# One more attention block turned by the DMA: block (0, 3), with another order of the first chunk and two copies on ScalarE

## The chip, the cores and the metric

The kernel runs on one core of a Trainium2 chip. The metric is the device time of one execution in microseconds (us). The kernel before has a median of 2323.25 us over three runs (2319.2 to 2325.48). Engines are named as in the profile: PE is TensorE (PEld its weight loads), DVE is VectorE, ACT is ScalarE, POOL is GpSimd, SP is SyncE, which issues most DMAs.

## The reference

Eight batches of 2496 tokens go through an attention without softmax; its output, 19968 rows of 256, goes through a mixture of eight experts with one expert for each row.

```python
scores = (1.0 / S) * np.matmul(z, z.transpose(0, 2, 1))   # z: 8 x 2496 x 64
attn = np.maximum(scores, 0.0) ** 2
x = u * np.matmul(attn, v)                                # u, v: 8 x 2496 x 256
logits = x @ w_gate                                       # 8 experts
...
h = np.maximum(xe @ w1[e], 0.0)                           # 256 -> 1024
ye = h @ w2[e]                                            # 1024 -> 256
out[mask] = gate_w[mask, None] * ye
```

Queries and keys are the same tensor z, so `attn` is symmetric: the part of keys a against queries b is the transpose of the part of keys b against queries a. All is float32 in and out.

## The kernel before, in words

The kernel has two parts, attention and then the experts. Only the attention is touched.

**Tiling.** A batch b (0 to 7) has five chunks c of 512 queries (the last has 448), and its keys are taken in ten pairs kp of 256 keys (two tiles of 128), so that key chunk cc = kp // 2. One step is (b, c, kp): `scores` makes the weights of 256 keys against the chunk's queries, and `weighted` multiplies them into the two PSUM accumulators of the chunk (`acc`, L343 to L346), with 12 products of 512 columns. Each float32 operand is split into a high part and a remainder (`hi`, `lo`; tiles `thi`, `tlo`), which is why a step needs three products for each pair of tiles.

**Where weights come from.** On and above the diagonal (cc >= c) four products of z make them (L306, L307, tile `ps_s`), ACT does Relu (L315) and Square (L316), and DVE makes `hi` (L317) and `lo` (L319). Below the diagonal (cc < c) nothing is computed again: the block stored by the earlier chunk is transposed. That is done in one of two ways, chosen by `by_dma`:

- By PE: the block is kept as float32 in a slot (tile `s`), eight transposes of 128x128 with the identity (L278) put it into PSUM, ACT makes `hi` (L279), DVE `lo` (L280).
- By the DMA: when the block is made, its 16-bit high halves are copied by ACT (L330) and its low halves by DVE (L331) into a ring of three tiles `th`, and SP issues a DMA_TRANSPOSE into the slot (L332). When it is used, ACT puts the high halves together (L263), DVE the low ones (L264), ACT makes `hi` (L265) and DVE `lo` (L266). No PE work is in it.

Before the change blocks (0, 1), (0, 2), (1, 2), (1, 3), (2, 3) and (3, 4) go by the DMA; (0, 3), (0, 4), (1, 4) and (2, 4) by PE. On the diagonal a chunk's second pair takes half of its weights from four PE transposes of the first (L312).

**Order.** `order_of` gives the order of the key pairs in a chunk. In the first chunk of batches 1 to 7 it is 0, 2, 6, 3, 7, 4, 8, 5, 9, 1: pairs that go by the DMA (2 to 5) take turns with the others, and the second diagonal pair (1) is last. Scores run three steps ahead of `weighted` (two in batch 0, whose first chunk has the order 0 to 9 and also splits z and v). The framework's scheduler then sets the order of each engine's instructions; engines keep it, so an instruction that waits holds up all behind it on its engine or queue. Other work goes in between: after a chunk `gate_x` makes x (L366, L376, L377), its halves are copied (L385, L386) and turned by four small DMA transposes on SP (L390), then the row goes to memory (L471). The last chunk of a batch also loads v of the next one (SP, L134) and splits it (ACT L139, DVE L140). Rings bound how far things run ahead: `ps_s` has two buffers, `tf` (the weights before their split) three, `thi` and `tlo` four each, slots six.

Of the kernel before, what the change touches and what calls it, by code (L numbers as in the profile page):

```python
# [47 lines left out]
def fused_kernel(ctx: ExitStack, tc: tile.TileContext, zt, ut, v, wg, wcat, out):  # L48
    nc = tc.nc
# [6 lines left out]
    NC_ = len(chunks)  # L56
# [38 lines left out]
    def ring_halves():  # L95
        return sb.tile([P, 4, QC], U16, name="th", tag="th", bufs=3)
# [128 lines left out]
    def order_of(b, c):  # L225

        kps = list(range(NKP))
        if b and c in (0, NC_ - 1):
            kps.append(kps.pop(1))
        elif 0 < c < NC_ - 1:  # L230
            kps.append(kps.pop(2 * c + 1))
        if b or c:

            ways = [[kp for kp in kps if kp // 2 > c and by_dma(c, kp // 2) == w] for w in (True, False)]
            at = [i for i, kp in enumerate(kps) if kp // 2 > c]
            mixed = []
            while any(ways):
                for w in ways:
                    if w:
                        mixed.append(w.pop(0))  # L240
            for i, kp in zip(at, mixed):
                kps[i] = kp
        return kps
# [3 lines left out]

    def by_dma(c, cc):

        return c < cc < NC_ - 1 and (c, cc) != (0, 3) or (c, cc) == (NC_ - 2, NC_ - 1)  # L250

    def scores(b, c, kp):
        q0, n = chunks[c]
        cc = kp // 2
        hi, lo = ring_hi(), ring_lo()
        if by_dma(min(c, cc), max(c, cc)) and cc < c:

            i, st = stored[b, cc, c]
            a = ring_f()
            st = st.rearrange("p k (i h j) q -> p h j (k i) q", i=2, h=2)  # L260
            dst = a.bitcast(U16).rearrange("p j (r q h) -> p h j r q", q=P, h=2)
            js = slice(kp % 2 * 2, kp % 2 * 2 + 2)
            nc.scalar.copy(dst[:, 1], st[:, 0, js])  # L263
            (nc.scalar.copy if c == NC_ - 1 else nc.vector.tensor_copy)(dst[:, 0], st[:, 1, js])  # L264
            nc.scalar.copy(hi[:, :, :n], a[:, :, :n])  # L265
            nc.vector.tensor_tensor(lo[:, :, :n], a[:, :, :n], hi[:, :, :n].bitcast(F32), op=ALU.subtract)  # L266
            if kp % 2:
                del stored[b, cc, c]
                free.insert(len(free) - len(weights), i)
            return hi, lo  # L270
# [15 lines left out]
        if cc > c:  # L286
            if kp % 2 == 0:
                i = free.pop(0)
                if by_dma(c, cc):
                    st = slot(i).bitcast(U16).rearrange("p (k r q) -> p k r q", k=2, q=P)  # L290
                else:
                    st = slot(i).rearrange("p (k i q) -> p k i q", k=2, i=2)
                stored[b, c, cc] = i, st
            a = ring_f() if by_dma(c, cc) else stored[b, c, cc][1][:, kp % 2]
        elif late and kp % 2 == 0:
            sd = ring_sd().bitcast(F32).rearrange("p s r -> p (s r)")[:, 0:2 * QC]
            a = stored[b, c, c] = sd.rearrange("p (i n) -> p i n", i=2)
        else:
            a = ring_f()
# [26 lines left out]
        if by_dma(c, cc):  # L326

            th = ring_halves().rearrange("p (i h) n -> p i h n", h=2)
            src = a.bitcast(U16).rearrange("p i (n h) -> p i n h", h=2)
            nc.scalar.copy(th[:, :, 0, :], src[:, :, :, 1])  # L330
            nc.vector.tensor_copy(th[:, :, 1, :], src[:, :, :, 0])  # L331
            nc.sync.dma_start_transpose(out=stored[b, c, cc][1][:, kp % 2], in_=th.rearrange("p i h n -> p (i h n)"))  # L332
        return hi, lo

# [486 lines left out]


    steps = [(b, c, kp) for b in range(B) for c in range(NC_) for kp in order_of(b, c)]
    LAST = len(steps) - 1
    LA = 3
    ZF, ZS = (0, 2), (1, 4)
    LP = 2
    ready, accs = {}, {}
    ready[0] = scores(*steps[0])
    split_v(0, 0)  # L830
    split_z(0, 1)
    pinned(lambda: warm_up(4))
    ready[1] = scores(*steps[1])
    pinned(lambda: warm_up(8))
    bg.extend([constants] + [nothing] * 6 + [gate_parts])
# [13 lines left out]
    for s, (b, c, kp) in enumerate(steps):  # L849
# [16 lines left out]
        def score():  # L866
            ready[ahead] = scores(*steps[ahead])
# [7 lines left out]
        if c == NC_ - 1 and b + 1 < B:  # L875

            for i in ((0, 1) if j == 0 else (j + 1,) if j < NKP - 1 else ()):
                fetch_v(b + 1, order_of(b + 1, 0)[i])
            if j:
                pinned(lambda: split_v(b + 1, order_of(b + 1, 0)[j - 1]))  # L880
# [122 lines left out]
```

## Time and profile before

| | |
|---|---|
| median of three runs | 2323.25 us |
| the profiled execution | 2324.7 us, span 2322.9 us |
| attention, up to about 1381 us | PE busy 1373.67, DVE 1078.71, ACT 982.21 us |
| experts, the 942 us after it | PE busy 905.19, DVE 553.28, ACT 483.08 us |
| DMA engines, mean share | 0.61 in the attention, 0.54 in the experts |
| PE transposes L278 | x512, 104.7 to 1368.8 us |
| DMA transposes into slots, L332 | x96 |

A batch takes about 170 us (batch 3 runs from about 522 to 692 us), its chunks 30 to 37 us each. The time of a matmul in a row of the profile (about 390 ns for 512 columns) is its latency; matmuls are started every 0.23 us and overlap. So the cost of a PE instruction is read from one start to the next. On ACT and DVE rows without idle time overlap as well, by about 0.1 us.

### The profile page before, as it was taken

The page shows a single profiled execution, that of the slowest core. Times are in us where ns is not written, and L with a number is a line of the kernel's source. Part 1 is how long each engine was busy: PE and PEld are TensorE (multiplying, and loading weights), DVE is VectorE, ACT ScalarE, POOL GpSimd, SP SyncE. Part 2 cuts the span into 40 slices and gives each one's busy share as a digit, 9 for nine tenths or more (in the row PEclk, how much of TensorE's full clock was granted, in tenths as well). Part 3 has the DMA queues.
Part 4 walks back from the last instruction along what each step waited for, and adds up shares of the span by engine and source line. Part 5 has one row for each costly group of instructions (what it writes and reads, how often), then busy time and mean ns, then how long its engine had stood idle before and what let it go on. Part 6 is the DMA issues. An engine that isn't in the chain of part 4 may idle for free.

```text
span 2322.9 us, 33688 instructions
## 1 busy us (share of the span) xinstructions
PE 2278.9 (98%) x12320; PEld 1925.6 (83%) x12320; DVE 1632.0 (70%) x2909; ACT 1465.3 (63%) x1985; POOL 625.7 (27%) x626
## 2 busy tenths in 40 slices
PE   9999999999999999999999989899999999999998
PEld 7888888888888888888888877688888888888887
DVE  8868868878778778877878766455566656657554
ACT  8768668677677777767776654355465555546454
POOL 1011111112102102102111244543445435345322
PEclk9999999999999999999999999899999999999999
DMA  6556656657567367467375484654566646457620
GB/s 163 104 92 135 97 86 135 93 95 134 85 105 132 80 116 121 79 118 125 79 114 95 121 176 89 189 123 131 154 152 173 176 128 207 134 146 194 151 89 29
DMA packets 454366, 287.31 MB, mean 124 GB/s; under 512 B 389100, under 2 KB 411130, under 8 KB 444976
## 3 DMA queue, kind: packets, MB, share of 16 engines
q1 hardware_dynamic: 422800, 165.98, 40.0%
q0 software_dynamic: 31392, 119.10, 17.6%
q8 instruction: 98, 1.61, 0.4%
q14 instruction: 76, 0.62, 0.1%
HBM read 149.79 MB, written 43.43 MB: 83 GB/s over the span
## 4 chain that ended last, share of the span: by engine, by line
PE 85%; issue 4%; DMA 3%; ACT 3%; DVE 2%; POOL 1%; another core or an unknown queue 1%; SPq 0%; POOLq 0%; ACTq 0%
PE ph L776 16%; PE acc L343 13%; PE acc L346 13%; PE acc L345 13%; PE y L799 11%; PE y L802 6%; PE ps_s L306 4%; PE ps_s L307 4%; DMA vr<-in_v_dram 2%; PE ps_s L278 2%; PE pt L398 1%; POOL out_dram L815 1%; PE ps_s L312 1%; DMA rows<-xrows,laidx 1%
## 5 line engine op out<-in xcount | busy, mean ns | idle before, releaser
L346 PE MATMUL acc<-thi,t 128*128 128x512 f32 (+1 forms) x1600 | 614.3, 386 | 0.0
L343 PE MATMUL acc<-thi,t 128*128 128x512 f32 (+1 forms) x1600 | 608.0, 392 | 1.1 <-issue 0.7
L345 PE MATMUL acc<-tlo,t 128*128 128x512 f32 (+1 forms) x1520 | 586.0, 386 | 0.1
L781 DVE SCALAR_TENSOR_TENSOR t<-ph,t 128x512 fp32r<-128x512 f32 (+1 forms) x328 | 220.3, 675 | 238.1 <-ACT t L780 192.5
L776 PE MATMUL ph<-thi,t 128*128 128x512 f32 (+2 forms) x1248 | 379.3, 361 | 3.8 <-issue 2.1
L780 ACT ACTIVATE t<-ph 128x512 fp32r<-128x512 f32 (+1 forms) x328 | 191.9, 591 | 289.1 <-PE ph L776 210.4
L346 PEld LDWEIGHTS acc<-thi,t 128*128 128x128 f32 x1600 | 300.2, 188 | 55.3 <-DVE t L140 0.6
L343 PEld LDWEIGHTS acc<-thi,t 128*128 128x128 f32 x1600 | 299.5, 188 | 54.4 <-DVE x L366 1.2
L345 PEld LDWEIGHTS acc<-tlo,t 128*128 128x128 f32 x1520 | 285.6, 188 | 50.8 <-DVE tlo L319 0.7
L476 POOL DMA_INDIRECT lst<-toks,posi x160 | 197.0, 1231 | 468.2 <-DVE posi L468 425.8
L799 PE MATMUL y<-t,t 128*128 128x512 f32 x1062 | 306.3, 397 | 13.5 <-DVE t L734 6.4
L776 PEld LDWEIGHTS ph<-thi,t 128*128 128x128 f32 x1248 | 226.1, 189 | 32.9 <-issue 2.9
L799 PEld LDWEIGHTS y<-t,t 128*128 128x128 f32 x1062 | 191.5, 191 | 48.7 <-ACT t L780 7.8
L776 PE MATMUL ph<-tlo,t 128*128 128x512 f32 (+2 forms) x624 | 225.6, 362 | 0.7 <-issue 0.7
L815 POOL DMA_INDIRECT out_dram<-tf,lfidx x136 | 143.7, 1057 | 273.4 <-DVE tf L813 245.5
L802 PEld LDWEIGHTS y<-t,t 128*128 128x128 f32 x1062 | 175.8, 190 | 35.2 <-DVE t L781 5.7
L802 PE MATMUL y<-t,t 128*128 128x256 f32 x1062 | 185.0, 283 | 3.6 <-DVE t L781 3.6
L315 ACT ACTIVATE tf<-ps_s 128x1024 f32<-128x1024 f32 (+1 forms) x145 | 133.8, 923 | 85.3 <-PE ps_s L307 43.3
L307 PE MATMUL ps_s<-t,t 128*128 128x512 f32 (+1 forms) x480 | 178.9, 376 | 0.0
L380 POOL MEMSET rows<- 128x64 int32 x40 | 6.8, 172 | 581.7 <-DMA xrows<-rows 359.6
L317 DVE CAST thi<-tf 128x1024 fp32r<-128x1024 f32 (+1 forms) x145 | 90.9, 627 | 102.3 <-ACT tf L316 94.5
L711 POOL DMA_INDIRECT rows<-xrows,lfidx x136 | 138.9, 1021 | 50.2 <-issue 38.3
(252 smaller groups left out, 4050.2 us busy)
## 6 DMA issues: line engine op xcount, KB each, us to landing
vr<-in_v_dram SPq DMA_DIRECT2D x80, 256.0 KB
xrows<-rows SPq DMA_DIRECT2D x32, 544.0 KB
u<-in_ut_dram SPq DMA_DIRECT2D x32, 512.0 KB
zr<-in_zt_dram SPq DMA_DIRECT2D x38, 256.0 KB
u<-in_ut_dram SPq DMA_DIRECT2D x8, 448.0 KB
xrows<-rows SPq DMA_DIRECT2D x8, 408.0 KB
rows<-th SPq DMA_TRANSPOSE x160
lst<-toks,posi POOLq DMA_INDIRECT x160
```

The costliest lines, as they stand in the source:

```text
L307: nc.tensor.matmul(ps[:, i, m:n], lhsT=hl_k, rhs=lh_q[:, m:n], start=False, stop=True)
L343: nc.tensor.matmul(acc[d][:, :n], lhsT=vh, rhs=hi[:, i, :n], start=first and i == 0, stop=False)
L345: nc.tensor.matmul(acc[d][:, :n], lhsT=vh, rhs=lo[:, i, :n], start=False, stop=False)
L346: nc.tensor.matmul(acc[d][:, :n], lhsT=vl, rhs=hi[:, i, :n], start=False, stop=last and i == 1)
L476: i = nc.gpsimd.indirect_dma_start(out=lst1, out_offset=bass.IndirectOffsetOnAxis(ap=posi[:m, j:j + 1], axis=0), in_=toks[:m, col + j:col ...
L711: nc.gpsimd.indirect_dma_start(out=xg[:, s, :], out_offset=None, in_=src, in_offset=bass.IndirectOffsetOnAxis(ap=lists[which]["idx"][:, s, ...
L776: nc.tensor.matmul(o, lhsT=w1[:, part, dd, fs], rhs=xx[:, dd, :n], start=p == 0, stop=p == 5)
L780: nc.scalar.activation(hh[:, :m], ph[:, :m], AF.Relu)
L781: nc.vector.scalar_tensor_tensor(hl[:, :m], ph[:, :m], 0.0, hh[:, :m].bitcast(F32), op0=ALU.max, op1=ALU.subtract)
L799: nc.tensor.matmul(y, lhsT=h[:, cs], rhs=w2[:, f % 2].rearrange("p i d -> p (i d)"), start=f == 0, stop=False)
L802: nc.tensor.matmul(y[:, 0:D], lhsT=h[:, cs], rhs=w2[:, f % 2, 0, :], start=False, stop=f == NF - 1)
L815: d = nc.gpsimd.indirect_dma_start(out=out, out_offset=bass.IndirectOffsetOnAxis(ap=lists[which]["idx"][:, s, t:t + 1], axis=0), in_=yo[:, ...
```

## The change

Three lines. Block (0, 3), made in the first chunk (pairs 6 and 7) and used in the fourth (pairs 0 and 1), goes by the DMA in all eight batches. The order of the first chunk in batches 1 to 7 becomes 0, 2, 3, 1, 4, 5, 8, 6, 9, 7: the second diagonal pair is fourth. And in those first chunks the low halves of pairs 2 and 3 (block (0, 1)) are copied by ACT and no longer by DVE.

```diff
     def order_of(b, c):
         kps = list(range(NKP))
-        if b and c in (0, NC_ - 1):
+        if b and c == 0:
+            return [0, 2, 3, 1, 4, 5, 8, 6, 9, 7]
+        if b and c == NC_ - 1:
             kps.append(kps.pop(1))
         elif 0 < c < NC_ - 1:
             kps.append(kps.pop(2 * c + 1))
...
     def by_dma(c, cc):
-        return c < cc < NC_ - 1 and (c, cc) != (0, 3) or (c, cc) == (NC_ - 2, NC_ - 1)
+        return c < cc < NC_ - 1 or (c, cc) == (NC_ - 2, NC_ - 1)
...
             nc.scalar.copy(th[:, :, 0, :], src[:, :, :, 1])
-            nc.vector.tensor_copy(th[:, :, 1, :], src[:, :, :, 0])
+            (nc.scalar.copy if b and c == 0 and kp < 4 else nc.vector.tensor_copy)(th[:, :, 1, :], src[:, :, :, 0])
```

Lines after the edit stand two further down: L278 is L280 in the changed kernel, L315 is L317, L330 is L332, L343 is L345. In its instruction lists, L333 is the copy of low halves on either engine.

Three places show how the instructions stand. First PE in batch 3, near the end of the third chunk, where the scores of the fourth chunk's first pair are due. Before:

```order
L345 MATMUL acc1_6029<-tlo_6134,t4_5252 128x512
L346 MATMUL acc1_6029<-thi_6133,t4_5252 128x512
L278 MATMUL ps_s_6263<-ident_97,s2_5314 128x128 x8
L343 MATMUL acc0_6028<-thi_6164,t4_5184 128x512
L345 MATMUL acc0_6028<-tlo_6165,t4_5184 128x512
```

In the change, at the end of the same chunk (no L278 stands between its products any more):

```order
L345 MATMUL acc1_6033<-thi_6202,t4_5333 128x512
L348 MATMUL acc1_6033<-thi_6202,t4_5333 128x512
L308 MATMUL ps_s_6447<-t2_5145 128x512
L309 MATMUL ps_s_6447<-t2_5146,t2_5145 128x512
L308 MATMUL ps_s_6447<-t2_5145 128x512
```

The eight transposes of block (0, 3) are gone; the next scores that PE makes are those of the fourth chunk's diagonal pair 6, which now stand before the third chunk's last products.

Second, ACT in the last part of the first chunk of batch 3, from the Relu of pair 8 on. Before (`s1_5475` holds pairs 8 and 9, `tf_5506` pair 5, `ps_s_5557` the diagonal pair 1, `sd_5659` the next chunk's diagonal, `s0_5259` block (0, 1)):

```order
L315 ACTIVATE s1_5475<-ps_s_5474 128x1024
L315 ACTIVATE tf_5506<-ps_s_5505 128x1024
L316 ACTIVATE s1_5475<-s1_5475 128x1024
L385 COPY th_5496<-x_5338 128x1024
L316 ACTIVATE tf_5506<-tf_5506 128x1024
L315 ACTIVATE s1_5475<-ps_s_5533 128x1024
L330 COPY th_5515<-tf_5506 128x2x512
L316 ACTIVATE s1_5475<-s1_5475 128x1024
L313 CAST thi_5555<-ps_s_5557 128x2x256
L315 ACTIVATE sd_5659<-ps_s_5658 128x1024
```

In the change (`s3_5480` holds pairs 8 and 9, `tf_5512` pair 6, `tf_5564` pair 7, `s0_5253` block (0, 1)):

```order
L317 ACTIVATE s3_5480<-ps_s_5479 128x1024
L317 ACTIVATE tf_5512<-ps_s_5510 128x1024
L318 ACTIVATE s3_5480<-s3_5480 128x1024
L387 COPY th_5501<-x_5336 128x1024
L318 ACTIVATE tf_5512<-tf_5512 128x1024
L317 ACTIVATE s3_5480<-ps_s_5539 128x1024
L332 COPY th_5521<-tf_5512 128x2x512
L317 ACTIVATE tf_5564<-ps_s_5563 128x1024
L265 COPY tf_5601<-s0_5253 128x1024
L318 ACTIVATE s3_5480<-s3_5480 128x1024
L318 ACTIVATE tf_5564<-tf_5564 128x1024
```

The half pair 1 has left this stretch and the whole pair 7 has come in, and a copy for the next chunk (L265) stands ahead of the Squares of pairs 9 and 7.

Third, ACT where the fourth chunk's last score (its second diagonal pair) is followed by the last chunk's first. Before (`ps_s_6589` is the first score of the last chunk, `s2_6487` block (3, 4)):

```order
L316 ACTIVATE tf_6551<-tf_6551 128x2x256
L279 CAST thi_6587<-ps_s_6589 128x2x448
L263 COPY tf_6760<-s2_6487 128x1024
L264 COPY tf_6760<-s2_6487 128x1024
L263 COPY tf_6813<-s2_6487 128x1024
L264 COPY tf_6813<-s2_6487 128x1024
L428 ACTIVATE ex_6361<-dl_6580 128x32
```

In the change (`ps_s_6581` is the first score of the last chunk, `s5_6479` block (3, 4)):

```order
L318 ACTIVATE tf_6543<-tf_6543 128x2x256
L265 COPY tf_6752<-s5_6479 128x1024
L266 COPY tf_6752<-s5_6479 128x1024
L265 COPY tf_6805<-s5_6479 128x1024
L266 COPY tf_6805<-s5_6479 128x1024
L281 CAST thi_6579<-ps_s_6581 128x2x448
L430 ACTIVATE ex_6353<-dl_6572 128x32
```

The four copies of block (3, 4), which wait for its DMA, now stand ahead of the cast that the last chunk's first products need.

## The prediction, made before the changed kernel ran

> **What bounds the kernel now.** I read the page's busy shares first, then busy time by stage, then the groups by line, then the order of time at the places that the edit touches.
>
> ```profile
> PE 2278.9 (98%) x12320; PEld 1925.6 (83%) x12320; DVE 1632.0 (70%) x2909; ACT 1465.3 (63%) x1985; POOL 625.7 (27%) x626
> PEclk9999999999999999999999999899999999999999
> 0.00:1381.00 1381.00, 1373.67 (x7477) 1148.62 (x7477) 1078.71 (x1867) 982.21 (x1128) 225.93 (x240) 1.00 0.61 111
> ```
>
> The third row is a window (columns: length, then busy time of PE, PEld, DVE, ACT, POOL, granted clock, DMA share, GB/s). In the attention PE idles 7.3 us of 1381 at full clock. Time falls here if PE work falls, provided the work put elsewhere hides behind PE. Batch 3 by chunks:
>
> ```profile
> 522.60:559.30 36.70, 36.70 (x188) 30.37 (x188) 28.44 (x48) 28.79 (x34) 7.27 (x5) 1.00 0.66 130
> 559.30:592.10 32.80, 32.80 (x175) 27.05 (x174) 28.95 (x51) 24.67 (x29) 4.40 (x5) 1.00 0.88 120
> 592.10:624.60 32.50, 32.50 (x182) 26.93 (x181) 27.04 (x49) 23.21 (x28) 5.04 (x5) 1.00 0.57 90
> 624.60:660.70 36.10, 36.10 (x206) 30.01 (x205) 23.71 (x40) 24.69 (x27) 4.16 (x5) 1.00 0.36 82
> ```
>
> PE is without a gap in all four; DVE and ACT have 4 to 12 us to spare in each.
>
> **What PE loses.** Block (0, 3) is two groups of eight transposes in each batch, 16 groups in all. One group in order of time, and ahead of it a step's 12 products:
>
> ```profile
> 643.93 0.39 PE L343 MATMUL acc<-thi,t 128*128 128x512 f32 x1
> ...
> 646.65 0.28 PE L306 MATMUL ps_s<-t 128*128 128x256 f32 x1
> ...
> 650.09 0.39 PE L346 MATMUL acc<-thi,t 128*128 128x512 f32 x1
> 650.32 1.03 PE L278 MATMUL ps_s<-ident,s 128*128 128x128 f32 x8
> 651.11 0.48 PE L343 MATMUL acc<-thi,t 128*128 128x512 f32 x1
> 651.42 0.40 PE L345 MATMUL acc<-tlo,t 128*128 128x512 f32 x1
> ```
>
> From start to start, 12 products take 2.72 us, one 0.227. From the group's start to the start of the second product after it are 1.10 us; less that product's 0.23 the group costs 0.87 us. 16 x 0.87 = 13.9 us less on PE. Nothing is added there.
>
> [...]
>
> **What ACT and DVE gain.** Durations of one, by shape:
>
> ```profile
> L263 ACT COPY tf<-s 128x1024 uint16<-128x1024 uint16 x96 | 126.7, 1359 | 31.7 <-DMA s<-th 17.9 <-DVE tlo L266 11.0 <-ACT thi L279 2.5
> L330 ACT COPY th<-tf 128x1024 uint16<-128x1024 uint16 x96 | 100.5, 1047 | 1.6 <-DMA s<-th 0.2
> L265 ACT CAST thi<-tf 128x1024 fp32r<-128x1024 f32 x80 | 83.0, 1056 | 56.6 <-PE acc L346 43.5 <-DVE tlo L266 5.0 <-DVE tf L264 4.3
> L279 ACT CAST thi<-ps_s 128x1024 fp32r<-128x1024 f32 x16 | 16.2, 1015 | 0.0
> L331 DVE COPY th<-tf 128x1024 uint16<-128x1024 uint16 x96 | 66.1, 689 | 0.6
> L264 DVE COPY tf<-s 128x1024 uint16<-128x1024 uint16 x80 | 57.9, 754 | 0.0
> ```
>
> *First chunk, batches 1 to 7.* ACT: high halves of pairs 6 and 7 (2 x 1.05), and low halves of pairs 2 and 3 (not seen on ACT; the nearest row is L330, the same shape and stride, 1.05 each): 4.2 us more. DVE: two low halves more, two fewer: 0. Is there room? ACT in batch 3, the stretch with its idle time and the one after it:
>
> ```profile
> 533.45 1.05 ACT L330 COPY th<-tf 128x1024 uint16<-128x1024 uint16 x1
> 540.85 1.03 ACT L315 ACTIVATE s<-ps_s 128x1024 f32<-128x1024 f32 x1 [6.35 <-PE ps_s L307]
> 542.68 1.06 ACT L316 ACTIVATE s<-s 128x1024 f32<-128x1024 f32 x1
> 548.32 0.58 ACT L313 CAST thi<-ps_s 128x512 fp32r<-128x512 f32 x1
> 551.98 0.58 ACT L315 ACTIVATE tf<-ps_s 128x512 f32<-128x512 f32 x1
> 554.87 0.63 ACT L316 ACTIVATE tf<-tf 128x512 f32<-128x512 f32 x1
> 540.80:560.00 19.20, 19.20 (x91) 16.01 (x90) 13.28 (x20) 18.07 (x20) 0.00 (x0) 1.00 0.38 75
> ```
>
> ACT idles 6.35 us because the scores of pair 8 come late in PE's order, then works 18.07 of 19.20 us. In the change's order the low halves of pairs 2 and 3 and the half pair 1 fall ahead of that hole, which covers them. In the tight stretch the half pair 1 goes (0.58 + 0.58 + 0.63 = 1.8), and pair 7 comes in whole (Relu 1.03, Square 1.06, high half 1.05: 3.1), pair 6 in the place of pair 5: 1.3 more, against 1.1 of idle time. What is pushed out at the end is work for the next chunk, which has 8 us to spare (second row by chunks, 32.80 - 24.67). Pair 9 is the tightest. From the start of pair 8's scores, PE's order is: scores of 8 and 6 (8 x 0.227 = 1.8), products of pair 5 (2.7), scores of 9 and 7 (1.8), products of 8 (2.7), a score (0.9), products of 6 (2.7), a score (0.9), then those of 9, at 13.6. ACT starts at 0.9 and has, in the order shown with the change, four times 1.0 to 1.1 up to the Square of 6 (6.1 with the row copy), Relu 9, high half 6, Relu 7 (9.2), L263's kind 1.36, Square 9: 11.7; DVE needs 3 x 0.69 more: 13.7. That is level with PE, and pair 7, in the same way, is 0.5 us ahead; ACT's rows overlap by about 0.1 us when none waits, which gives back near 1. I take 0. Ends: 0 (PE has no gap there to lose) and all 4.2 us uncovered, 7 x 4.2 = 29.4.
>
> *Fourth chunk, all batches.* Per pair ACT has L263 and L265 for L279 (1.36 + 1.06 - 1.02 = 1.4), DVE L264 more (0.75; the subtraction costs the same from either memory). 2.8 and 1.5 us per batch, beside 5.5 to 12.4 us of spare time on either engine in the third and fourth rows by chunks (the fourth chunk's first scores run in the third's stretch). PE, which runs ahead there, needs none of it sooner. 0; ends 0 and 8 x 2.8 = 22.4.
>
> *Batch 0, first chunk.* Here the low halves stay on DVE, and nothing moves away:
>
> ```profile
> 19.60:39.60 20.00, 20.00 (x88) 15.94 (x87) 19.28 (x27) 17.84 (x22) 0.00 (x0) 1.00 0.95 197
> ```
>
> DVE is busy 19.28 of 20.00 us. Two low halves are 2 x 0.69 = 1.4 us on the path; ACT's 2.1 just fit its 2.2 us of idle time. +1.4; ends 0 and 1.4 + 2.1 = 3.5.
>
> **What the DMA gains.** 16 transposes. The rows of SP's issue and of the waits on them:
>
> ```profile
> L332 SPq DMA_TRANSPOSE s<-th x96: 1317/2074/5038, 16.8 to 1333.8; - x96
> ACT tf L263 <- DMA s<-th: 17.9, 8, 4.3
> ACT t L139 <- DMA vr<-in_v_dram: 28.7, 12, 5.6
> ```
>
> SP issues one in 2.07 us: 4.1 us per batch of 170. Behind the two on SP's queue stand u, z and the next chunk's transposes, for which later chunks wait; in batch 0 also the last v. The first chunk's end and the second's start have a free DMA (0.38 in the 540.80 row). The result is read two chunks later. 0; the existing waits bound it: 28.7 us if v came late as often again.
>
> **The fourth chunk's end.** The cast and the subtraction of a first score of the last chunk:
>
> ```profile
> L279 ACT CAST thi<-ps_s 128x896 fp32r<-128x896 f32 x48 | 42.6, 902 | 48.9 <-PE acc L346 44.7 <-PE ps_s L278 4.2
> L280 DVE TENSOR_TENSOR tlo<-ps_s,thi 128x896 fp32r<-128x896 f32 x48 | 52.1, 1087 | 55.1 <-ACT thi L279 46.0 <-issue 9.1
> ```
>
> There ACT's order puts four copies of block (3, 4) ahead of the cast that the last chunk waits for. Each batch waits once for that block's DMA (17.9 us over 8, longest 4.3). The block is made earlier than before (its scores start in the third chunk now), so the wait should shrink. Once PE ends the fourth chunk's last diagonal transposes, it has 2.72 us of products and 0.87 of the last chunk's first transposes; ACT has 0.58 + 0.58 + 0.63 before it reaches the copies, 1.8 us ahead of the transposes' end. 8.6 us of PE work (2.72 + 2.27 + 0.87 + 2.72) follow. Copies (4 x 1.36), cast (0.90) and subtraction (1.09) take 7.4 us and end 1.8 + 8.6 - 7.4 = 3.0 us ahead. 0; ends: all of PE's idle time in the attention gone, -7.3, or +1.3 per batch (below).
>
> **Sum.** -13.9 + 1.4 = -12.5 on the profiled 2324.7 gives 2312.2. That execution lies 1.45 over the median, so 2311 for the median of 2323.25.
>
> **Rivals.**
> - *ACT becomes the bound of the first chunk* (slower). For it: 18.07 of 19.20 us, and weights that come level with PE; whatever ACT is late there, PE is late. Against it: the hole of 6.35 us. Price: 29.4 uncovered, 2323.25 - 12.5 + 29.4 = 2340; it cancels the gain from 12.5 / 7 = 1.8 us per batch, and decides for slower from 2.8.
> - *The copies at the fourth chunk's end hand it back* (no change). With a wait of 4.3 us in every batch the first weights come 4.3 - 3.0 = 1.3 us late, 10 in all: 2321. Against it: the mean wait was 2.2 us, and the block is earlier.
> - *The DMA is late instead* (no change): 0.88 of the DMA is used in the second chunk, 0.95 in batch 0. If a sixth more transposes bring a sixth more of both waits (46.6 / 6 = 7.8): 2319. [...]
> - *Waits go too* (faster than forecast): the earlier block (3, 4) frees ACT, and with it v's queue; PE's idle 7.3 us goes: 2304.
>
> **How the numbers follow.** A run of this kernel spreads by 0.3% (7 us), about what can be told from no change. Forecast 0.56, waits go too 0.10, copies 0.13, DMA 0.09, ACT 0.12. Faster by over 0.3% (under 2316.3): 0.56 + 0.10 = 0.66. Within: 0.13 + 0.09 = 0.22. Slower: 0.12. The range leaves out the slower case and the ends of the others: 2302 (13.9 + 7.3 below the median) to 2322 (just past the copies). The forecast's own is 2305 to 2316.
>
> **What would show it.** L280 with 384 instructions for L278's 512, L334 with 112 for 96; PE still without gaps in the attention, which ends some 12 us earlier, with batches 1 to 7 near 168.3 us (1.74 less) and batch 0 hardly shorter. Wrong, if ACT's rows end the idle time of L343 or L345 at the end of first chunks, if the cast L281 does at the start of last ones, or if the waits on `th` or v grow by more than 8 us.

## The result, and the profile after

The change made the kernel slower: 2335.98 us (median of 14 runs, 2326.24 to 2343.96) against 2323.64 us for the kernel before on the same chip, a ratio of 1.0051, 95% interval 1.0036 to 1.0067. Forecast were 2311 us, with a range of 2302 to 2322. The profiled execution of the changed kernel took 2336.84 us with a span of 2335.1.

First the page's busy times, and then the attention as one window, of after and of before (columns: length, then PE, PEld, DVE, ACT, POOL, granted clock, DMA share, GB/s):

```profile
PE 2276.6 (97%) x12192; PEld 1916.9 (82%) x12192; DVE 1643.8 (70%) x2927; ACT 1510.3 (65%) x2031; POOL 623.6 (27%) x626
0.00:1393.70 1393.70, 1370.98 (x7338) 1138.59 (x7339) 1087.23 (x1876) 1025.72 (x1170) 225.34 (x240) 0.99 0.68 115
```

```profile
0.00:1378.10 1378.10, 1371.36 (x7465) 1147.28 (x7466) 1075.81 (x1858) 980.30 (x1125) 225.93 (x240) 1.00 0.61 111
```

The 128 transposes are gone (12320 to 12192), and yet the attention ends 15.6 us later, at 1393.7. The experts take 941.4 us after it (944.8 before), so between these two executions the whole loss lies in the attention. PE's idle time there rose from 6.7 to 22.7 us, and its busy time fell by only 0.4 us: rows that start late one by one, or at a lower clock, count as busy (in the 3.40 us from 382.5 on, at a granted clock of 0.50, nine rows make PE busy for all of it). Lost time is therefore better read from one start to the next. I added up by how much each interval between two starts exceeds that of an undisturbed neighbour (0.227 us for 512 columns, 0.203 for 448, 0.119 for 256, 0.109 for a transpose), where it is over 0.06 us:

| us lost by PE | before | after |
|---|---|---|
| first chunks, batch 0 / batches 1 to 7 | 3.1 / 1.3 | 4.4 / 10.6 |
| second and third chunks, batches 1 to 7 | 5.2 | 5.6 |
| fourth chunks, batches 1 to 6 / batch 7 | 4.7 / 2.6 | 15.7 / 10.2 |
| last chunks, batches 1 to 7 | 8.3 | 5.9 |
| whole attention | 26.8 | 54.2 |

(Batch 0's other chunks, 1.5 and 1.8 us, are in the last row alone. A stall at the end of a fourth chunk reaches into the last one, so these two rows are best read together: 15.6 us before, 31.8 after.) So 27.4 us of new lost time stand against 13.9 us of saved work: +13.5 of the 15.6 us. Not all of it is waiting. In the change's attention the granted clock of PE is 0.50 in four stretches, 20.5 us in all (rows in the last section), and there is no such stretch in the attention of the trace of before; the slower starts in them, waits aside, make some 7 of the 54.2 us. Who waits is in the table of waits of the changed kernel (us in all, times, longest):

```profile
ACT tf L265 <- DMA s<-th: 36.1, 8, 12.3
ACT t L139 <- DMA vr<-in_v_dram: 18.8, 12, 4.1
ACT th L332 <- DMA s<-th: 17.2, 7, 3.9
DVE th L333 <- DMA s<-th: 13.5, 6, 3.5
PE ps_s L308 <- ACT tf L317: 5.7, 5, 2.2
PE acc L345 <- ACT thi L281: 4.6, 3, 2.7
```

The first row was 17.9 us with a longest of 4.3, the third 0.2, the fourth not there. The wait for v fell from 28.7 to 18.8. In the groups by line, the cast and the subtraction of the last chunk's first scores show the same:

```profile
L282 DVE TENSOR_TENSOR tlo<-ps_s,thi 128x896 fp32r<-128x896 f32 x48 | 51.5, 1086 | 80.3 <-ACT thi L281 80.3
L281 ACT CAST thi<-ps_s 128x896 fp32r<-128x896 f32 x48 | 43.4, 903 | 55.2 <-PE ps_s L280 31.8 <-PE acc L348 22.7 <-issue 0.7
```

DVE waits 80.3 us for the cast L281, where it was 46.0.

**End of a fourth chunk.** Batch 2 in order of time, ACT and then PE (start, length, in brackets the idle time before and what ended it):

```profile
482.19 0.63 ACT L318 ACTIVATE tf<-tf 128x512 f32<-128x512 f32 x1
488.94 1.35 ACT L265 COPY tf<-s 128x1024 uint16<-128x1024 uint16 x1 [6.12 <-DMA s<-th]
492.55 1.32 ACT L266 COPY tf<-s 128x1024 uint16<-128x1024 uint16 x1
493.74 0.89 ACT L281 CAST thi<-ps_s 128x896 fp32r<-128x896 f32 x1
```

```profile
482.12 1.03 PE L280 MATMUL ps_s<-ident,s 128*128 128x128 f32 x8
491.64 0.39 PE L348 MATMUL acc<-thi,t 128*128 128x512 f32 x1
494.68 0.47 PE L345 MATMUL acc<-thi,t 128*128 128x448 f32 x1 [2.65 <-ACT thi L281]
495.81 1.97 PE L280 MATMUL ps_s<-ident,s 128*128 128x128 f32 x8 [0.66 <-DVE tlo L282]
```

The first transposes of the last chunk are in PSUM at 483.2 us. ACT could cast them at once, but block (3, 4)'s four copies stand ahead of the cast in its list, and they wait 6.12 us for the block's DMA. PE has finished the fourth chunk at 491.9 and then waits. Before, one cast stood ahead of the copies:

```profile
481.60 0.89 ACT L279 CAST thi<-ps_s 128x896 fp32r<-128x896 f32 x1
483.49 1.35 ACT L263 COPY tf<-s 128x1024 uint16<-128x1024 uint16 x1 [1.00 <-DMA s<-th]
```

Count both from the chunk's first product (456.4 us before, 460.2 after). ACT came to the copies after 26.1 us and found the block there after 27.1; in the change it comes after 22.6 and finds it after 28.7. In all of batches 0 to 6 ACT came after 25.9 to 26.1 us, and comes after 22.6 to 23.9, one cast sooner and in a chunk that takes 31.7 us for 34.3 where PE does not wait. The first copy starts after 27.9 us before and 26.5 in the change (means). So the block is not later there, and the wait still grows from 1.9 to 3.4 us in the mean. Only in batch 7 does the block itself come late, after 34.7 us for 29.0 (there the copies stood ahead of both casts before, too). SP in batch 2, after and then before:

```profile
464.27 12.52 SPq L392 DMA_TRANSPOSE rows<-th  x4
476.90 8.57 SPq L334 DMA_TRANSPOSE s<-th  x2
```

```profile
470.68 5.23 SPq L390 DMA_TRANSPOSE rows<-th  x4
476.08 1.79 SPq L332 DMA_TRANSPOSE s<-th  x1
479.16 2.91 SPq L332 DMA_TRANSPOSE s<-th  x1
```

SP takes 12.52 us over four small transposes that took 5.23, and then 8.57 over the two of the block that took 4.7. All the same it is done with them 25.3 us after the chunk's first product, for 25.6 before, because it comes to them earlier. Over all, the median issue of one into a slot rose from 2.07 to 2.98 us.

**First chunks.** Batch 2 again, ACT and the PE row that waits for it:

```profile
379.25 1.04 ACT L332 COPY th<-tf 128x1024 uint16<-128x1024 uint16 x1 [3.95 <-DMA s<-th]
380.21 1.02 ACT L317 ACTIVATE tf<-ps_s 128x1024 f32<-128x1024 f32 x1
```

```profile
381.28 0.50 PE L308 MATMUL ps_s<-t,t 128*128 128x512 f32 x1 [2.18 <-ACT tf L317]
```

A copy into the ring of three `th` waits until an earlier DMA transpose has read its buffer. The Relu behind it is late, the PSUM buffer of the score comes free late, and PE waits 2.18 us.

**The end of batch 7.** There PE stops, with nothing in the trace that it waits for:

```profile
1350.90 0.39 PE L347 MATMUL acc<-tlo,t 128*128 128x512 f32 x1 [1.04 <-issue]
1353.96 0.58 PE L348 MATMUL acc<-thi,t 128*128 128x512 f32 x1 [2.67 <-issue]
1356.05 0.58 PE L345 MATMUL acc<-thi,t 128*128 128x512 f32 x1 [1.50 <-issue]
```

```profile
1344.00:1350.00 6.00, 5.75 (x33) 4.74 (x32) 1.98 (x7) 0.74 (x2) 3.85 (x5) 1.00 1.65 74
1350.00:1356.00 6.00, 0.97 (x2) 0.57 (x2) 0.00 (x0) 0.00 (x0) 0.00 (x0) 0.65 1.11 237
1356.00:1362.00 6.00, 5.82 (x18) 3.86 (x18) 0.00 (x0) 4.89 (x5) 0.00 (x0) 0.50 0.09 19
1362.00:1368.00 6.00, 5.80 (x35) 5.01 (x34) 5.09 (x13) 2.64 (x5) 2.52 (x3) 0.99 0.65 217
```

In 6 us PE starts two products; then it runs at a granted clock of 0.50 (18 of its rows in 6 us, 33 in the window two before). It happens beside eight gathers of token rows for the experts that POOL issues from 1337.9 to 1349.7 (L713) and the transposes of block (3, 4).

### The profile page after: what moved, and what is told of

It reads as the page before. It is cut to its first block, busy times and chain, and to the rows that moved or that the text cites. A ratio compares the mean times of both kernels' runs of the same rounds, so it can differ in the third digit from the quotient of the medians.

```text
span 2335.1 us, 33566 instructions
## 1 busy us (share of the span) xinstructions
PE 2276.6 (97%) x12192; PEld 1916.9 (82%) x12192; DVE 1643.8 (70%) x2927; ACT 1510.3 (65%) x2031; POOL 623.6 (27%) x626
## 3 DMA queue, kind: packets, MB, share of 16 engines
q8 instruction: 97, 1.59, 0.3%
## 4 chain that ended last, share of the span: by engine, by line
PE 78%; DMA 7%; issue 5%; DVE 4%; ACT 3%; POOL 1%; another core or an unknown queue 1%; SPq 0%; POOLq 0%; DVEq 0%; ACTq 0%
PE ph L778 16%; PE acc L345 12%; PE acc L348 12%; PE acc L347 11%; PE y L801 11%; PE y L804 6%; DMA s<-th 5%; PE ps_s L308 4%; PE ps_s L309 4%; PE ps_s L280 1%; PE pt L400 1%; DVE tlo L321 1%; DMA rows<-xrows,laidx 1%; ACT tf L265 1%; ACT tf L266 1%
## 5 line engine op out<-in xcount | busy, mean ns | idle before, releaser
L345 PE MATMUL acc<-thi,t 128*128 128x512 f32 (+1 forms) x1600 | 604.8, 392 | 6.5 <-ACT thi L281 4.6
L345 PEld LDWEIGHTS acc<-thi,t 128*128 128x128 f32 x1600 | 301.3, 189 | 62.3 <-ACT thi L281 6.5
L317 ACT ACTIVATE tf<-ps_s 128x1024 f32<-128x1024 f32 (+2 forms) x161 | 149.3, 932 | 72.0 <-DVE tlo L316 42.1
L265 ACT COPY tf<-s 128x1024 uint16<-128x1024 uint16 x112 | 147.7, 1363 | 36.1 <-DMA s<-th 36.1
L319 DVE CAST thi<-tf 128x1024 fp32r<-128x1024 f32 (+2 forms) x161 | 103.0, 640 | 91.4 <-ACT tf L318 87.8
```

The source lines that it names most:

```text
L317: nc.scalar.activation(a[:, :, m:n], ps[:, :, m:n], AF.Relu)
L345: nc.tensor.matmul(acc[d][:, :n], lhsT=vh, rhs=hi[:, i, :n], start=first and i == 0, stop=False)
```

## Experiments

Three theories. **A**: ACT waits for two DMAs, for the ring `th` in first chunks and for block (3, 4) at the end of fourth chunks, and holds up PE. **B**: ACT has too much to do in the first chunk. **C**: the load of the DMA engines as such. The runs were made on four chips, on which the kernel before took 2333.6, 2324.1, 2295.2 and 2319.2 us; so ratios are to the kernel before on the same chip. Forecasts in us are for a kernel before of 2323.6 us. "Lost" is PE's lost time in the attention, added up as above, with its part in the first and fourth chunks of batches 1 to 7. The expectations quote a narrower count, each interval against the median of its own kind, by which the change lost 8.1, 20.6 and 3.0 us in first, fourth and last chunks.

**Parts of the change: `block_only` and `order_only`.**

```diff
# block_only: only by_dma is changed; the first chunk's old order, which hangs on by_dma, is written out
+            return [0, 2, 6, 3, 7, 4, 8, 5, 9, 1]
-        return c < cc < NC_ - 1 and (c, cc) != (0, 3) or (c, cc) == (NC_ - 2, NC_ - 1)
+        return c < cc < NC_ - 1 or (c, cc) == (NC_ - 2, NC_ - 1)
# order_only: only the order and ACT's low halves are changed
+            return [0, 2, 3, 1, 4, 5, 8, 6, 9, 7]
+            (nc.scalar.copy if b and c == 0 and kp < 4 else nc.vector.tensor_copy)(th[:, :, 1, :], src[:, :, :, 0])
```

> Block (0, 3) goes by the DMA as in the change, but the first chunk keeps its old order (0, 2, 6, 3, 7, 4, 8, 5, 9, 1) and DVE keeps its low-half copies. Theory A, two waits of ACT on DMAs make the loss (for a free `th` tile in first chunks, some 8 us over batches 1 to 7, and for block (3, 4) at the end of fourth chunks, some 14 us more than before): five DMA pairs follow each other in this order, so the ring of three `th` tiles runs dry as soon or sooner; 2330 to 2350 us. Theory B, ACT's extra work in the first chunk makes it: 2.1 us less ACT work in each batch, so most of the loss goes; 2312 to 2326. Theory C, the DMA engines' load as such makes it: as the change, 2333 to 2340.

> The new order and ACT's low halves of pairs 2 and 3 stay, block (0, 3) is transposed by PE as before the change. Theory A: no third user of the ring in the second half of the first chunk and no more DMA work; 2316 to 2328 us, about the kernel before. Theory B: ACT still has 2.1 us more in each first chunk, so part of the loss stays; 2328 to 2340. Theory C: as before, 2321 to 2327.

Measured: `block_only` 1.0055 (1.0037 to 1.0073), lost 55.9 (first 3.4, fourth 28.7). `order_only` 1.0029 (1.0013 to 1.0045), lost 45.2 (first 8.5, fourth 10.5, last chunks 16.0). Waits of ACT in `block_only`, then in `order_only`:

```profile
ACT tf L265 <- DMA s<-th: 35.6, 8, 13.8
ACT th L332 <- DMA s<-th: 5.9, 6, 2.4
```

```profile
ACT t L139 <- DMA vr<-in_v_dram: 35.9, 12, 10.5
ACT tf L265 <- DMA s<-th: 19.4, 9, 5.2
```

`block_only` fits A and C alike. The long wait for block (3, 4) comes with its one edit, without the new order of the first chunk. That edit also changes ACT's order at the fourth chunk's end, though: all eight batches of `block_only` have the four copies ahead of both casts, while in `order_only` seven have a cast first, as before. So these two runs do not part the load of the transposes from ACT's order. `order_only` came out slower than A had it (2316 to 2328 us, a ratio of up to 1.002) and inside B's range: the order alone loses 7.7 us more than the kernel before in last chunks, where v of the next batch is late, and 7.2 more in first chunks, mostly in small pieces (2.8 us of it are waits for DVE's splits L319 and L321, none for the ring).

**Each wait taken away: `own_halves` and `pin`.** `own_halves` puts block (0, 3)'s halves into a free slot. `pin` holds the scores of the last chunk's pairs 6 and 7 in their place, so that the casts L281 come ahead of the four copies.

```diff
# own_halves
+    spare = []
-            th = ring_halves().rearrange("p (i h) n -> p i h n", h=2)
+            if (c, cc) == (0, 3):
+                if kp % 2 == 0:
+                    spare.append(free.pop(0))
+                    spare.append(slot(spare[0]).bitcast(U16).rearrange("p (k n) -> p k n", k=2))
+                th = spare[1][:, kp % 2].rearrange("p (i h n) -> p i h n", i=2, h=2)
+                if kp % 2:
+                    free.insert(len(free) - len(weights), spare[0])
+                    spare.clear()
+            else:
+                th = ring_halves().rearrange("p (i h) n -> p i h n", h=2)
# pin
-            pinned(score) if s <= NKP else score()
+            pinned(score) if s <= NKP or (steps[ahead][1] == NC_ - 1 and steps[ahead][2] // 2 == NC_ - 2) else score()
```

> The change, with the halves of block (0, 3) put into a free slot in place of the ring `th`, so that ACT and DVE need not wait there for an earlier transpose; the same work and the same DMAs. Theory A: the waits of ACT's L332 for the ring in first chunks go, and 8 us with them; 2325 to 2331 us. Theory B: no change, 2333 to 2339. Theory C: no change, 2333 to 2339.

> The change, with the scores of the last chunk's pairs 6 and 7 held in program order, so that ACT's four copies of block (3, 4) come behind the casts of the last chunk's first scores. Theory A: the stalls of PE at the start of last chunks (about 14 us more than before, two thirds of them in batch 2 and batch 7) go; 2319 to 2327 us. Theory B and theory C: PE would stall elsewhere for the same load; 2332 to 2338.

Measured: `own_halves` 1.0058 (1.0036 to 1.0080), lost 55.5 (first 1.9, fourth 31.7). `pin` 0.9977 (0.9961 to 0.9993), lost 44.6 (first 17.6, fourth 13.1, of which 9.4 in batch 7). Waits of ACT in `own_halves` (its lines stand one to ten further down: L266 is the change's L265, L342 its L332), then in `pin`:

```profile
ACT tf L266 <- DMA s<-th: 44.6, 8, 14.3
ACT th L342 <- DMA s<-th: 4.2, 4, 1.7
```

```profile
ACT th L332 <- DMA s<-th: 15.5, 10, 3.4
ACT th L387 <- DMA s<-th: 7.3, 3, 3.8
```

`own_halves` removes the ring's wait and is no faster than `block_only` on this chip, where A had 1.001 to 1.003: the time goes to the other wait, ACT waits 44.6 us for block (3, 4). `pin` removes that one in batches 1 to 6 and is faster, as only A had it (for C 1.004 to 1.006); its first chunks lose 17.6 us, with 22.8 us of ACT's waits for the ring (L332 and, for the rows of x, L387) where the change has 17.2. Theory B as the main cause falls here: in `own_halves` ACT has all the work of the change in the first chunk, and PE loses 1.9 us there.

**Both together, and controls: `own_halves_pin`, `own_halves_pin_b7`, `before_pin`, `low_dve`.** The first has both edits above. The second, besides, leaves block (3, 4) of batch 7 to PE. `before_pin` is the kernel before with the edit of `pin`. `low_dve` is the change with all low halves on DVE.

```diff
# own_halves_pin_b7, beside own_halves_pin (by_dma takes b as well there)
-        return c < cc < NC_ - 1 or (c, cc) == (NC_ - 2, NC_ - 1)
+        return c < cc < NC_ - 1 or (c, cc) == (NC_ - 2, NC_ - 1) and b < B - 1
# low_dve, beside the change
-            (nc.scalar.copy if b and c == 0 and kp < 4 else nc.vector.tensor_copy)(th[:, :, 1, :], src[:, :, :, 0])
+            nc.vector.tensor_copy(th[:, :, 1, :], src[:, :, :, 0])
```

> The change, with both waits attacked at once: block (0, 3)'s halves lie in a free slot and not in the ring of three, and the scores of the last chunk's pairs 6 and 7 are held in their place, so that the four copies of block (3, 4) come behind the casts L282 of the last chunk's first weights. Theory A (the loss is two waits of ACT on DMAs): each edit alone took away its own stall (first chunks 8.1 to 0.6 us; fourth chunks 20.6 to 9.0), so together about 0.6 + 9 + 3 us are left over batches 1 to 7 beside the 11 us that the kernel before has: the 13.9 us that PE saves show nearly whole, ratio 0.993 to 0.996 to the kernel before. Theory B (ACT has too much work in the first chunk): pin's 13 us in first chunks stay, ratio 0.998 or more. Theory C (the load of the DMA engines as such): the waits come out somewhere else, ratio 0.998 or more.

> own_halves_pin, but in batch 7 alone block (3, 4) is turned by PE, since there the weight loads of the experts share the DMA engines with its two transposes (12.4 and 15.7 us, where other batches show 4 to 9), and the two earlier runs that held the casts or not lost 8 to 12 us in that one chunk. 16 transposes of PE come back, 2 x 0.87 = 1.7 us. Theory A: batch 7's fourth chunk has no stall, 7.8 - 1.7 = 6 us faster than own_halves_pin, ratio 0.991 to 0.994. If those 7.8 us are not due to block (3, 4) (the weight loads hit another wait, or the end of the attention waits for v or rows): equal to own_halves_pin or up to 2 us slower.

> The kernel before with only the scores of the last chunk's pairs 6 and 7 held in their place. It has 4.1 us of stall at the end of its fourth chunks in batches 1 to 7, of which the wait on block (3, 4) is a part. Theory A: that wait does little harm there, so 0 to 4 us faster, ratio 0.998 to 1.000: holding the casts is not by itself what makes `pin` 0.23 per cent faster than the kernel before. If holding alone brings as much as in the change (18 us, 0.8 per cent): ratio 0.993 or less.

> The change without its third line: the low halves of pairs 2 and 3 are copied by DVE again, so ACT has 2.1 us less to do in each first chunk and DVE 1.4 us more. Theory A: ACT and DVE wait for the ring of three in first chunks as before, 8 us of stall there and 20 at the fourth chunks' ends stay, ratio 1.003 to 1.007. Theory B (ACT's extra copies make the first chunk slow): the first chunks' 8 us go, ratio 1.002 or less.

| | ratio (95%) | lost | first | fourth | in batch 7 |
|---|---|---|---|---|---|
| own_halves_pin | 0.9948 (0.9931 to 0.9966) | 42.9 | 11.3 | 11.8 | 8.1 |
| own_halves_pin_b7 | 0.9980 (0.9960 to 1.0000) | 40.7 | 9.9 | 13.9 | 10.2 |
| before_pin | 0.9968 (0.9943 to 0.9993) | 35.8 | 11.0 | 4.0 | 0.8 |
| low_dve | 1.0132 (1.0105 to 1.0159) | 78.6 | 14.9 | 36.2 | 11.7 |

What ACT waits for in `own_halves_pin`:

```profile
ACT s L318 <- DMA s<-s: 20.5, 6, 6.7
ACT t L139 <- DMA vr<-in_v_dram: 18.1, 8, 3.5
ACT th L342 <- DMA s<-th: 5.8, 5, 2.5
```

The wait for block (3, 4) is gone and that for the ring is 5.8 us. A Relu now waits for the slot that held the halves (first row), and PE loses 7.3 us in second chunks for 1.9. `own_halves_pin` is faster than the kernel before by 0.5% and, by the two ratios, than the change by about 1%, as theory A has it. But its first chunks lose 11.3 us where 0.6 were expected, as much as those of `before_pin`: holding the scores has a price there. And its profiled attention is no shorter than that of before (1380.6 for 1378.1 us, on two chips): 13.9 us less work, 16.1 more lost. The difference of these two traces lies in the experts (924.4 for 944.8 us; PE loses 17.8 for 31.4 in their first 200). That may be the chip: all four runs here have experts of 924 to 936 us, `low_dve` without held scores too (931.8), and the kernel before has no trace on it. `before_pin` came out between its two forecasts, 0.3% faster with no block moved, so part of the 0.5% may be the held scores. What the block by the DMA is worth shows best beside it, with the same hold on the same chip: attention 7.5 us shorter (1380.6 for 1388.1), about half of the 13.9, since PE loses 7.1 more. `low_dve` speaks against B a second time: with less work on ACT its first chunks lose 14.9 us, and its ratio is 0.8% above the change's. In `own_halves_pin_b7` the expected 6 us were not won, it is 7 us slower than `own_halves_pin`. PE's stop in batch 7 is there without block (3, 4)'s transposes: 3.5 us from 1334.4 with nothing to wait for, and then, at a clock of 0.50, 2.0 us of waiting for the subtraction L283.

**The stop in batch 7: gathers three steps later.** `late_x` on the change, `before_late_x` on the kernel before, `own_halves_pin_late_x` on `own_halves_pin`.

```diff
-             NKP + 2: [lambda: load_x(0)],
-             NKP + 1: [lambda: load_x(1)],
-             NKP - 1: [lambda: load_w(1, 0), lambda: turn_x(0)],
-             NKP - 3: [lambda: take_gates(0)],
-             NKP - 4: [lambda: load_x(2)],
-             NKP - 5: [lambda: turn_x(1)],
+             NKP - 1: [lambda: load_w(1, 0), lambda: load_x(0)],
+             NKP - 2: [lambda: load_x(1)],
+             NKP - 4: [lambda: turn_x(0)],
+             NKP - 5: [lambda: take_gates(0), lambda: load_x(2)],
+             NKP - 6: [lambda: turn_x(1)],
```

> The change, with one other edit in the last batch alone: the gathers of the first two token blocks of the experts (load_x, L713) are issued three steps later, behind block (3, 4)'s two transposes and not beside them. In the change's trace PE stops at 1349.5 us in batch 7 for 6 us with nothing that it waits for, one instruction every 0.70 us, while those gathers and transposes fill the DMA engines; then the clock is granted at 0.50 for 8 us, and ACT's wait on block (3, 4) is 12.3 us there. The same stop, at 1334 to 1350 us, is in all five traces with block (0, 3) by the DMA and DVE's low halves as in the change, and not in that of the kernel before. Theory A (wait of ACT on block (3, 4), with the gathers beside the transposes as its cause in batch 7): the stop is gone, batch 7's fourth chunk 42.9 us before the edit is then 34 to 37, ratio to the kernel before 1.001 to 1.004 (the change 1.0051). Rival (the stop comes from something else in the last batch, code loading by itself for one): the stop is still there, ratio as the change or slower.

> The kernel before with the gathers of the experts' first two token blocks three steps later, as a control. It has no stop of PE in batch 7, so nothing is there to win: ratio 0.999 to 1.002 if the later gathers cost nothing at the start of the experts, up to 1.004 if the first turns of x then come late.

> own_halves_pin with the gathers three steps later in the last batch. There PE stops from 1336 to 1343 us in the same way (7.0 us, one instruction every 0.70 us), with the clock at 0.50 up to 1346. Theory A with the gathers as the cause: those 8 us go, ratio 0.990 to 0.994 to the kernel before, attention ends near 1373 us for 1380.6. Rival (another cause): the stop stays, ratio 0.995 or more.

Measured, on the chip of 2295 us: 1.0118 (1.0094 to 1.0143), 1.0041 (1.0026 to 1.0056) and 0.9954 (0.9940 to 0.9967). None of the three has a stop; the third loses 31.0 us in all, 0.7 in batch 7's fourth chunk. In the first two ACT waits 16.2 and 18.9 us for the turned x at the very end, a price of the edit itself. None of the three ratios lies in the range that A had. Since the kernels with the gathers in their old place had no trace on this chip yet, edit and chip were mixed up.

**On one chip: `before_again`, `after_again`, `late_x2`, `own_halves_pin_late_x2`.** The first two are the kernels themselves. The others move the gathers by two steps and the turn of x by one:

```diff
+             NKP: [lambda: load_x(0)],
+             NKP - 1: [lambda: load_w(1, 0), lambda: load_x(1)],
+             NKP - 2: [lambda: turn_x(0)],
+             NKP - 3: [lambda: take_gates(0)],
```

> The kernel before once more, as a look at its trace on the same chip as the three that follow. The chip of the last three runs gave 2295.3 us for it, where the others gave 2323.6 to 2333.6, and the experts had next to no idle time of PE there. Theory A: attention within 5 us of 1378.1 if the chip matters to the experts alone; no stop of PE in batch 7, as in its first trace.

> The change once more, on the chip of before_again and the two that follow. Theory A (two waits of ACT on DMAs, and in the last batch the gathers beside block (3, 4)'s transposes): the order of instructions is the cause, not the chip, so attention again 12 to 18 us longer than in before_again, ACT's wait L265 on block (3, 4) 30 to 40 us over 8, that on the ring of three near 17 us, ratio 1.003 to 1.008; if this chip is like the first two, PE's stop at 1350 us in batch 7 as well. Rival (the loss hangs on the chip): attention within 5 us of before_again's.

> The change with the experts' first gathers two steps later in the last batch, and the turn of x one step later only (late_x moved that by three, and ACT then waited 16.2 us for it at the end). Whether the gathers cause PE's stop could not be told from late_x, since no run with the stop was made on its chip. With after_again beside it: if the gathers are the cause and after_again shows the stop, late_x2 shows none and its batch 7 is 4 to 8 us shorter than after_again's. If the chip decides, both show it or neither. ACT's wait for the turned x is the risk: 0 to 10 us at the end of batch 7.

> All three edits to the change: block (0, 3)'s halves in a free slot, the four copies behind the casts at the last chunk's start, the gathers two steps later in the last batch (the turn of x one). Theory A: what is left of PE's idle time in the attention is near 31 us, as in own_halves_pin_late_x (before 27, the change 54), so attention is 8 to 12 us shorter than in before_again, ratio 0.991 to 0.996. If the copies, the ring or the gathers were not what the change lost to: ratio 0.998 or more.

| | ratio (95%) | attention | lost | first | fourth | stop of PE |
|---|---|---|---|---|---|---|
| before_again | | 1374.4 | 23.1 | 1.3 | 7.4 | none |
| after_again | 1.0024 (1.0013 to 1.0036) | 1379.3 | 40.3 | 2.8 | 23.1 | 6.3 at 1335.1 |
| late_x2 | 1.0039 (1.0023 to 1.0054) | 1389.7 | 50.5 | 2.9 | 19.0 | 8.0 at 1367.3 |
| own_halves_pin_late_x2 | 1.0039 (1.0020 to 1.0057) | 1391.7 | 53.9 | 9.2 | 4.4 | 7.9 at 1350.9 (late starts from 1345.1) |

The waits of `after_again` on the same two DMAs:

```profile
ACT tf L265 <- DMA s<-th: 31.0, 8, 11.9
ACT th L332 <- DMA s<-th: 5.6, 4, 2.4
```

The change loses on this chip as well, but half as much. The attention is 4.9 us longer, where A had 12 to 18 and the rival, that the loss hangs on the chip, up to 5: the wait for block (3, 4) is there again, as A had it, and the ring's is small. The stop is in the same place, as the last gather is issued, and it moves with the gathers, which run from 1324.0 to 1334.7 us in `after_again`, from 1354.0 to 1371.5 and from 1334.1 to 1356.1 in the other two. These two also wait 11.4 and 13.9 us for the turned x, and missed what was expected of them (for the second 0.991 to 0.996).

**Last, three on the chip of 2295 us: `own_halves_pin_again`, `own_halves_pin_late_x_again`, `own_halves_pin_late_x1`.** The first two repeat. The last moves the two gathers by one step (`NKP + 1` and `NKP`) and nothing else.

> own_halves_pin once more (block (0, 3)'s halves in a free slot, the four copies behind the casts), beside the two that move the gathers of the last batch. Theory A: 0.993 to 0.998 to the kernel before on any chip, the larger where the DMA is quick and the change itself loses little; PE's stop in batch 7 is there once, at 1336 us or near it.

> own_halves_pin_late_x once more, now beside own_halves_pin on one chip. If the gathers beside the DMA transposes cause the stop of 6 to 8 us and the three later steps keep them apart: 4 to 10 us faster than own_halves_pin, ratio 0.990 to 0.995. If the stop only moves with the gathers, as in late_x2 and own_halves_pin_late_x2, or ACT waits for the turned x: equal to own_halves_pin or up to 10 us slower.

> own_halves_pin with the gathers one step later only and the turn of x where it was. If the stop needs the gathers beside the transposes: less of both together than in own_halves_pin, stop 2 to 6 us, no wait for x, ratio 0.992 to 0.996. If it moves with the gathers: as own_halves_pin.

Measured: 0.9940 (0.9927 to 0.9953), 0.9948 (0.9935 to 0.9961) and 0.9979 (0.9961 to 0.9997), with 36.9, 29.1 and 32.8 us lost. In the last two PE waits another 4.5 and 11.3 us behind the attention's last product, for the subtraction (L771) of the experts' first block. `own_halves_pin_again` has the stop in the expected place, but short:

```profile
1336.11 0.40 PE L358 MATMUL acc<-thi,t 128*128 128x512 f32 x1 [0.27 <-issue]
1337.64 0.39 PE L355 MATMUL acc<-thi,t 128*128 128x512 f32 x1 [1.13 <-issue]
```

Two starts from 1335.4 on take 2.2 us, just behind the last gather (issued up to 1335.2). With the gathers three steps later there is none. So the stop goes with the gathers, and is short on this chip; what makes it stays open, and moving the gathers wins nothing that can be told. `own_halves_pin` is the best version, faster than the kernel before on the two chips on which it ran.

## Why the prediction was wrong, point by point

*The saving on PE, -13.9: right.* From start to start, all 128x128 transposes of the attention take 62.3 us before and 48.4 in `own_halves_pin`, 13.9 less.

*The first chunk on ACT, 0, and batch 0, +1.4: right in size.* `own_halves`, with all of ACT's new work, loses 1.9 us in seven first chunks. That the new order is not free there in every kernel shows in `order_only`, which loses 8.5 us with less work on ACT. Batch 0's first chunk lost 1.3 us more (3.1 to 4.4). The rival of ACT as the bound gave the nearest time (2340), but not by its mechanism.

*"What the DMA gains ... 0; the existing waits bound it": the first step that failed.* It priced two waits that were there and left out a third that was nearly empty (0.2 us), that for a free buffer of the ring. Six pairs of a first chunk pass through the three buffers for four before, and a copy now comes while the DMA still reads. The wait became 17.2 us on ACT and 13.5 on DVE, and PE lost 9.3 us more in seven first chunks. `own_halves` removes just this, but by itself wins no time, since the other wait grows.

*"The fourth chunk's end ... The block is made earlier than before, so the wait should shrink. 0": the second, and the larger.* The block did come earlier, by 1.4 us in the chunk in the mean of batches 0 to 6. But the wait that the sum used (2.2 us in the mean, 4.3 at most) had been measured where ACT came to the copies 25.9 to 26.1 us into the chunk, in seven of eight batches, behind a cast. In the change ACT comes there after 22.4 to 23.9 us, because the copies stand ahead of both casts and the chunk itself is 2.6 us shorter. The sum took the new order for the slack, and the old one for the wait. Measured were 36.1 us of waits for 17.9, and PE lost 18.6 us more in seven fourth chunks (16.2 together with last chunks). The slack worked out there held: with 3.0 us of it, waits of 3.3, 3.9, 4.8 and 6.1 us (batches 1, 3, 6 and 2) should cost 0.3, 0.9, 1.8 and 3.1, and the chunks became 0.1, 0.7, 1.5 and 2.8 us longer. Only the wait's size was wrong. `pin` shows that it no longer costs anything in batches 1 to 6 once the casts come ahead of the copies. In batch 7 the block lands 5.7 us later than before, so there the DMA was put too low as well. Both waits stood among the signs of being wrong, priced at nothing in the sum and at 10 and 7.8 us in two separate rivals; they came together.

*Not foreseen: the stop of PE in batch 7.* It is in 7.6 of those 18.6 us (2.6 to 10.2); how much of these is the stop and how much block (3, 4), for which ACT waits 12.3 us there, the change's own trace does not part.

`pin`, with the same blocks by the DMA and an attention 11.4 us shorter than that of `own_halves` on the same chip (1383.0 for 1394.4), shows that what decided was not the transposes' own time but who stands behind them. That `own_halves_pin` beats the kernel before because of these blocks is not shown.

Open: why the start of the experts is quicker on some chips and perhaps with held scores, what makes `low_dve` so much slower (a part is its clock, at 0.50 for 37.5 us of its attention, for 20.5 in the change), why `order_only` loses time in first chunks, and why the ring's wait is small on one chip.

## What to carry to other kernels

A transfer taken off the bound engine is not free when buffers or queues are shared (here ACT's wait for the ring went from 0.2 to 17.2 us): before pricing it at nothing, list every ring that its source and its target pass through and what stands behind each wait in the engine's order, even where the wait is near zero now. A wait has two ends: what is waited for may come earlier, and the wait still grows if the engine that waits comes earlier yet (here by 1.4 us and by 2.0 to 3.4, and a mean wait of 1.9 us became 3.4). So before a measured wait is carried over to a new order, work out both times from one fixed point. And when two waits feed one engine, removing one may only lengthen the other (in `own_halves` that for block (3, 4) is 44.6 us, in the change 36.1), so try them apart and together.

## What the runs showed of the hardware

PE can stop with no wait that the trace shows: its starts come 0.7 to 3.1 us apart, for 6.6 us in the change's trace from 1349.5 us. Off the chip of 2295 us it came in all ten traces with block (0, 3) by the DMA, for some 3.5 to 8 us, and for some 4 us in `before_pin`; on that chip in one of its six, for 2.2 us. In `low_dve` it takes 5.2 us from 1367.7:

```profile
1369.18 0.27 PE L280 MATMUL ps_s<-ident,s 128*128 128x128 f32 x1 [1.24 <-issue]
1371.29 0.27 PE L280 MATMUL ps_s<-ident,s 128*128 128x128 f32 x1 [1.84 <-issue]
```

One packet of an instruction queue lies between 1345 and 1360 us of the change's trace:

```profile
q8 instruction: 1, 0.02, 0.5%
```

This queue, q8, has 97 packets for 1.59 MB in the whole trace, 16.4 KB each. That the packet has to do with the stop was not shown: the kernel before has 98 of them, one between 1330 and 1350 us too, and no such stop.

Time without work on PE can cost more than its own length. In the change's attention the granted clock fell to 0.50 at 1351.9 us for 10.2 us, six of them after the stop, and also behind ordinary waits, for 3.4 us each from 382.5 (the wait of 2.18 us in a first chunk), 495.1 (that of 2.65 us at the end of a fourth) and 1184.6 us; products of 512 columns then start 0.43 us apart (1357.3 to 1359.1 us) for 0.227. It stayed at 1.00 behind the wait of 1.64 us at 901.5. The 3.4 us ahead of the first fall and the 3.4 us behind it:

```profile
379.10:382.50 3.40, 1.22 (x5) 1.03 (x6) 3.20 (x4) 3.25 (x4) 0.00 (x0) 1.00 0.99 197
382.50:385.90 3.40, 3.40 (x9) 2.62 (x9) 2.39 (x4) 3.40 (x4) 0.00 (x0) 0.50 0.88 168
```

In none of the four cases were the 3.4 us ahead of the fall without work: PE's rows fill 0.8 to 1.7 of them.

Chips differ more than this change: the kernel before took 2295.2 to 2333.6 us on four of them, and on the quickest PE loses some 4 us in the first 200 of the experts (`own_halves_pin_again`) where the same kernel on another loses 17.8.
